# Full-row matmuls in the first token product, and one value product in each double step without scores

## The chip, the cores and the metric

The kernel runs on one core of a Trainium2 chip. The metric is the device time of one execution in microseconds (us), the median of three runs; lower is better. Five engines work side by side, each through its own queue in order: PE (TensorE, matmuls; the profile lists its weight loads as PEld), DVE (VectorE), ACT (ScalarE), POOL (GpSimd) and SP, which here only issues DMAs.

## The reference

Attention with the heads mixed before and after the softmax, then one token-and-channel MLP block on its output. Four batches, 12 heads, 448 positions, 64 elements a head, 768 channels.

```python
scores = scale * np.matmul(q, k.transpose(0, 1, 3, 2))
scores = np.einsum('bhij,hg->bgij', scores, w_pre)
attn = softmax(scores)                                  # over j, with 1e-9 added to the sum
attn = np.einsum('bhij,hg->bgij', attn, w_post)
x = np.matmul(attn, v)                                  # laid out as (batch, position, 768)
h = np.maximum(x.transpose(0, 2, 1) @ w_tok1, 0.0) @ w_tok2      # 448 -> 256 -> 448
u = x + h.transpose(0, 2, 1)
out = u + np.maximum(u @ w_ch1, 0.0) @ w_ch2                     # 768 -> 1536 -> 768
```

All data are float32.

## The kernel before

**Attention.** The 448 rows of a batch are cut into tiles T of 120, 120, 120 and 88 rows, 16 tiles in all. A tile's scores (`qk`, six calls a tile, two heads each) go to SBUF, and DMAs regroup them (`regroup`, to tile `r`) so that one group holds ten rows of all heads. A *step* takes two groups through `pre` (head mixing), `mx` (negated row maximum on DVE), `ex` (exponentials on ACT, two halves), `rec` (reciprocal on DVE, then two multiplications on POOL, lines 196 and 199), `post` (head mixing after the softmax, PE) and `turn` (a 32 by 32 transpose on DVE into the tile's `at` buffer, of which there are two). When all steps of a tile are turned, three calls of `av(T, hp)` make its value product on PE, with a copy on ACT (line 247), an addition on POOL (line 249) and a store.

**Double steps.** The main loop runs over 45 double steps J. Each issues six stages of steps that overlap: `post` and `turn` of steps `pa`, `pb`, `ex` and `rec` of `ea`, `eb`, `pre` and `mx` of `na`, `nb`. A planner (lines 469 to 488) sets ahead of time which `qk` and which `av` calls belong to which J: `score[J]` and `value[J]`. The engines' order is written out by hand and has two forms, chosen by the line quoted below. With scores in J, or with neither scores nor values, the first form is taken (lines 526 to 559): both `post` first, `av` last. With values but no scores the second form is taken (lines 561 to 582): `post(pa)`, `pre(na)`, then `av` between the exponentials of `eb` and `rec(eb)`, and then `post(pb)` and `pre(nb)`.

```python
        if qs or not vs:
```

The products `qk`, `post` and `av` share two PSUM buffers of the tag `w`; `pre` has two of its own. A product can begin only when the reader of the buffer's former content (the copy on ACT, or `turn` on DVE) is done.

Scores end at J = 38. Of the last double steps, 38 holds two value products of tile 12 and two score calls, 39 holds nothing, 40 one value product of tile 13, 41 two, 42 nothing, 43 one of tile 14 and 44 two. Tile 15 has its value products behind the loop.

**Weight conversion.** The MLP weights come as float64 bits and are split on the chip into a high and a low float32r part. `tok_tick` does the first token weight during J = 29 to 40. `cv_tick` does the rest unit by unit from J = 41 on (52 units; lines 432, 436 and 442 on DVE, 408 and 423 on ACT, 414 on POOL, 440 on POOL or, in the channel stage, on DVE). It is spread over the token stage and the first batch of the channel stage.

**Token stage.** For each batch: `tok1(b)`, `tr(b + 1)`, `tok2(b)`. `tr` transposes x on PE and splits it on ACT (line 606) and DVE (line 608, eight instructions a batch) into `xn` high and low. `tok1` has four groups (two halves of the channels, two of the 256 hidden units). A group is three times three matmuls of 128 rows (lines 616 to 618: high by high, high by low, low by high) for rows 0 to 383, and two matmuls for the last 64 rows: the tile `xn[0][:, 3]` holds the low part of those rows in partitions 0 to 63 and the high part in 64 to 127, and `w[0][:, 3]` holds the high weights twice, so line 630 makes high by high and high by low in one matmul of 128 rows. Line 631 makes low weights by high x from partitions 64 to 127 alone. `relu_split` follows on ACT (line 612) and DVE (line 613). `tok2` adds its product to x on DVE (line 649).

**Channel stage.** For each batch and each of 12 chunks c: `ch1` (18 matmuls), `relu_split` (lines 612 and 613, tiles `rh` and `rl`), three conversion units in batch 0, and `ch2` of the chunk before (18 matmuls), which reads `rl`.

Of the kernel before, what the change touches and what calls it, by code (L numbers as in the profile page):

```python
# [14 lines left out]
ALU = mybir.AluOpType  # L15
# [21 lines left out]
def attn_mixer_kernel(  # L37
# [12 lines left out]
    nc = tc.nc  # L50
    f32 = lambda ap: ap.bitcast(F32)
# [11 lines left out]
    def en(name, **kw):  # L63
        p = tc.alloc_tile_pool(name=name, reuse_waits="tile", **kw)
        opens[name] = p
        return p
# [27 lines left out]
    for b in range(B):  # L94
        for t in range(4):
            n = IT[t][1]
# [4 lines left out]
    NT = len(first)  # L101
# [28 lines left out]
    def pair(tag, name):  # L130
        return (ps if tag == "pre" else ps_w).tile([128, 2, 512], F32, tag=tag, bufs=2, name=name)
# [150 lines left out]
    for i in range(WARM):  # L282
        p = pair("w", "pw")
# [3 lines left out]
    for x in range(2):  # L287
        ps_ = slice(64 * x, 64 * x + 64)
        nc.vector.tensor_tensor(
            out=kpre[ps_, :60].rearrange("p (i g) -> p i g", i=5),  # L290
            in0=kcat[0][ps_, :12].unsqueeze(1).to_broadcast([64, 5, H]),
            in1=mask[0][ps_, 5 * x:5 * x + 5].unsqueeze(2).to_broadcast([64, 5, H]), op=ALU.mult,
# [3 lines left out]
    for s in range(2):  # L296
        ps_ = slice(64 * s, 64 * s + 64)
        for hf in range(2):
            nc.gpsimd.tensor_tensor(
                out=kpost[ps_, 32 * hf:32 * hf + 30].rearrange("p (g i) -> p g i", g=6),  # L300
                in0=kcat[1][ps_, 12 + 6 * hf:18 + 6 * hf].unsqueeze(2).to_broadcast([64, 6, 5]),
                in1=mask[1][ps_, 5 * s:5 * s + 5].unsqueeze(1).to_broadcast([64, 6, 5]), op=ALU.mult,
# [9 lines left out]
    prep = {}  # L312
# [5 lines left out]
    a1 = en("a1", bufs=1, side="right")  # L318
    cvt = en("cvt", bufs=2, side="right")
    prep["t1"] = [a1.tile([128, JT, DT], F32R, name=f"t1{i}") for i in range(2)]  # L320
    toks = [(w_t1[:, 512 * j:512 * (j + 1)], DT, [y[:, j, :] for y in prep["t1"]]) for j in range(JT)]
    tok_t = {}

    def tok_tick(t):
        i, odd = divmod(t, 2)
        if odd == 0:
            if 0 <= i < len(toks):
                src, n, _ = toks[i]
                r = cvt.tile([128, n, 2], I32, tag="r", bufs=3, name="tk_r")
                nc.sync.dma_start(out=r, in_=src.rearrange("p (n two) -> p n two", two=2))  # L330
                tok_t[i] = [r]
            i -= 2
            if 0 <= i < len(toks):
                r, g, a = tok_t[i]
                nc.scalar.copy(out=toks[i][2][0], in_=a)
            i += 1
            if 0 <= i < len(toks):
                g = cvt.tile([128, toks[i][1]], F32, tag="g", name="tk_g")
                nc.scalar.activation(out=g, in_=f32(tok_t[i][0])[:, :, 1], func=ACTF.Abs)
                nc.gpsimd.tensor_scalar(  # L340
                    out=g, in0=g, scalar1=MAG_MIN, scalar2=MAG_MAX, op0=ALU.max, op1=ALU.min,
                )
                tok_t[i].append(g)
        else:
            i -= 1
            if 0 <= i < len(toks):
                r, g = tok_t[i]
                a = cvt.tile([128, toks[i][1]], F32, tag="a", name="tk_a")
                ri, gi, ai = [y.bitcast(U32) for y in (r, g, a)]
                nc.vector.tensor_scalar(  # L350
                    out=gi, in0=gi, scalar1=3, scalar2=0x3FFFFFFF,
                    op0=ALU.logical_shift_left, op1=ALU.bitwise_and,
                )
                nc.vector.scalar_tensor_tensor(
                    out=ai, in0=ri[:, :, 1], scalar=0xC0000000, in1=gi, op0=ALU.bitwise_and, op1=ALU.bitwise_or,
                )
                nc.vector.scalar_tensor_tensor(
                    out=ai, in0=ri[:, :, 0], scalar=29, in1=ai, op0=ALU.logical_shift_right, op1=ALU.bitwise_or,
                )
                tok_t[i].append(a)  # L360
            i -= 1
            if 0 <= i < len(toks):
                hi, lo = toks[i][2]
                nc.gpsimd.tensor_tensor(out=lo, in0=tok_t.pop(i)[2], in1=f32(hi), op=ALU.subtract)

    def open_prep():
        close("cvt")
# [79 lines left out]
    def cv_tick(k, eng=nc.gpsimd):  # L447
        for _ in range(k):
            i = cv_pos[0]
            if i >= cv_lim[0]:  # L450
                return
            if i + 5 < len(units):
                cv_load(i + 5)
            cv_step(i, eng)
            if 0 <= i + 2 < len(units):
                cv_clamp(i + 2)
            if 0 <= i + 3 < len(units):
                cv_abs(i + 3)
            cv_pos[0] += 1
# [4 lines left out]
    sf = [f // 2 for f in first]  # L464
# [3 lines left out]
    value = {J: [] for J in range(-2, ND)}  # L468
    for T in range(NT - 1):
        J = (sl[T] + 1) // 2  # L470
        n = min(3, sf[T + 2] // 2 - J)
        for hp in range(3):
            value[J + min(hp, n - 1)].append((T, hp))
    for h in range(HP):
# [4 lines left out]
    for T in range(2, NT):  # L479
        hi = (sf[T] - 8) // 2  # L480
        lo = max((sl[T - 2] - 8) // 2 + 1 + (T == 4), hi - 2)
# [16 lines left out]
    for b in range(1, B):  # L498
        for h in range(0, HP, 2):
            J = uses[4 * b, 0] - 5 + h // 2  # L500
# [9 lines left out]
    for J in range(-2, ND):  # L510
# [49 lines left out]
        else:  # L560
# [20 lines left out]
            if na:  # L581
                ex(na, 0)
        tok_tick(J - JC)
        if J >= ND - 4:
            cv_tick((2, 1, 1, 1)[J - ND])
# [8 lines left out]
    def tr(b, hfs=(0, 1)):  # L594
        x = XR[b]
        xn = XN.get(b) or [a2.tile([128, JT - i, DM], F32R, tag=f"xn{i}", bufs=1, name=f"xn{i}") for i in range(2)]
        for hf in hfs:
            for j in range(JT):
                p = pst.tile([128, 512], F32, tag="tr", name="tr")
                for d in range(3):  # L600
                    nc.tensor.transpose(
                        out=p[:, 128 * d:128 * d + 128], in_=x[hf][:, d, min(128 * j, 320):min(128 * j, 320) + 128],
                        identity=prep["ident"],
                    )
                cs = slice(384 * hf, 384 * hf + 384)
                nc.scalar.copy(out=xn[0][:, j, cs], in_=p[:, :384])
                lo_t, r = (xn[1][:, j, cs], 0) if j < 3 else (xn[0][:64, 3, cs], 64)
                nc.vector.tensor_tensor(out=lo_t, in0=p[r:, :384], in1=f32(xn[0])[r:, j, cs], op=ALU.subtract)
        XN[b] = xn

    def relu_split(p, h, l):
        nc.scalar.activation(out=h, in_=p, func=ACTF.Relu)  # L612
        nc.vector.scalar_tensor_tensor(out=l, in0=p, scalar=0.0, in1=f32(h), op0=ALU.max, op1=ALU.subtract)  # L613

    def mm3(p, a, x, first, last):
        nc.tensor.matmul(out=p, lhsT=a[0], rhs=x[0], start=first, stop=False)  # L616
        nc.tensor.matmul(out=p, lhsT=a[0], rhs=x[1], start=False, stop=False)  # L617
        nc.tensor.matmul(out=p, lhsT=a[1], rhs=x[0], start=False, stop=last)  # L618

    def tok1(b):  # L620
        xn = XN[b]
        h1 = [a3.tile([128, 2, DM], F32R, tag=f"h1{i}", bufs=1, name=f"h1{i}") for i in range(2)]
        for hf in range(2):
            for m in range(2):
                p = psa.tile([128, 512], F32, tag="t", bufs=4, name="pt1")
                cs = slice(384 * hf, 384 * hf + 384)
                w = [y[:, :, 128 * m:128 * m + 128] for y in prep["t1"]]
                for j in range(3):
                    mm3(p[:, :384], [y[:, j] for y in w], [y[:, j, cs] for y in xn], j == 0, False)
                nc.tensor.matmul(out=p[:, :384], lhsT=w[0][:, 3], rhs=xn[0][:, 3, cs], start=False, stop=False)  # L630
                nc.tensor.matmul(out=p[:, :384], lhsT=w[1][64:, 3], rhs=xn[0][64:, 3, cs], start=False, stop=True)
                relu_split(p[:, :384], h1[0][:, m, cs], h1[1][:, m, cs])
                if b == hf == m == 0:
                    tr(0, (1,))
                if hf + m == 1 if b == 0 else hf == 0:
                    cv_tick(1)
        H1[b] = h1
# [49 lines left out]
    for b in range(B):  # L687
        tok1(b)
        if b + 1 < B:
            tr(b + 1)  # L690
        tok2(b)
# [93 lines left out]
```

## Time and profile before

| | |
|---|---|
| median of 3 runs | 773.65 us (773.21 to 775.1) |
| profiled execution, whole / its span | 778.99 us / 777.2 us |
| granted TensorE clock over the span | 0.999 |
| PE / DVE / ACT / POOL busy share of the span | 97% / 55% / 42% / 44% |
| attention (to about 337 us) / token stage / channel stage (from about 416 us) | 337 / 79 / 361 us |

The busy shares are means over stages that differ: DVE, ACT and POOL are near their limits up to about 500 us and nearly idle behind it. A matmul's duration includes its run through the array, so matmuls overlap, and what one costs is the distance of its start to the next start, not its duration. The idle time in square brackets at the end of a row is that of the row's engine just before it, with what ended it.

### The profile page before, as it was taken

How to read it: one execution, taken by the hardware profiler on the slowest of the kernel's cores; microseconds unless marked ns; L12 is line 12 of the kernel's file. 1: busy time of each engine (PE TensorE's matmuls, PEld its weight loads, DVE VectorE, ACT ScalarE, POOL GpSimd, SP SyncE). 2: the span in 40 equal slices, each digit the busy share in tenths (PEclk: the TensorE clock that was granted, in tenths of full speed). 3: DMA queues.
4: the chain of work that ended last, by engine and by line, in shares of the span. 5: the costliest groups of instructions: out<-in, count | busy, mean ns of one | idle time of the engine just before them, and what ended most of it. 6: DMA issues, size and time to landing. Idle time of an engine off the chain costs nothing.

```text
span 777.2 us, 21834 instructions
## 1 busy us (share of the span) xinstructions
PE 753.9 (97%) x9209; PEld 565.3 (73%) x9209; DVE 430.9 (55%) x749; ACT 329.9 (42%) x732; POOL 339.9 (44%) x342
## 2 busy tenths in 40 slices
PE   7899999999999998899999999999999999999997
PEld 2354565455555455578888999999999999999997
DVE  3776667666767978687999999620004000230002
ACT  2777777677777775455453445300002000200000
POOL 3676677667767778856668676100000000000000
PEclk9999999999999999999999999999999999999999
DMA  6776676466747633735656565330003000010001
GB/s 165 251 234 214 215 219 210 158 220 205 223 168 235 204 140 144 243 110 183 237 178 195 166 180 163 143 142 1 1 1 141 1 1 0 1 72 1 0 1 72
DMA packets 62755, 105.66 MB, mean 136 GB/s; under 512 B 21012, under 2 KB 49601, under 8 KB 62145
## 3 DMA queue, kind: packets, MB, share of 16 engines
q1 hardware_dynamic: 62160, 103.35, 41.0%
q8 instruction: 73, 1.20, 0.6%
q10 hardware_dynamic: 400, 0.87, 0.4%
q14 instruction: 26, 0.20, 0.1%
q0 software_dynamic: 96, 0.03, 0.0%
HBM read 49.18 MB, written 16.52 MB: 85 GB/s over the span
## 4 chain that ended last, share of the span: by engine, by line
PE 87%; DVE 6%; POOL 2%; ACT 2%; DMA 1%; issue 1%; SPq 0%; DVEq 0%; POOLq 0%; ACTq 0%
PE av L240 9%; PE post L208 9%; PE pc L616 8%; PE pc L617 8%; PE pc L618 8%; PE po L616 8%; PE po L617 8%; PE po L618 8%; PE qk L143 7%; PE pre L165 7%; DVE at L222 3%; PE pt L616 3%; PE pt L617 2%; PE pt L618 2%; POOL e L199 1%
## 5 line engine op out<-in xcount | busy, mean ns | idle before, releaser
L613 DVE SCALAR_TENSOR_TENSOR rl<-pc,rh 128x448 fp32r<-128x448 f32 x48 | 29.8, 622 | 227.4 <-ACT rh L612 227.4
L199 POOL TENSOR_TENSOR e<-e,sm 128x896 f32<-128x896 f32 x90 | 151.4, 1682 | 7.0
L222 DVE STREAM_TRANSPOSE at<-post 128x1024 f32<-128x1024 f32 (+1 forms) x98 | 112.0, 1150 | 66.5 <-PE post L208 66.3
L612 ACT ACTIVATE rh<-pc 128x448 fp32r<-128x448 f32 x48 | 26.1, 543 | 242.0 <-PE pc L618 242.0
L149 ACT COPY s<-qk 120x896 f32<-120x896 f32 (+1 forms) x91 | 82.2, 906 | 81.5 <-PE qk L143 80.1
L182 ACT ACTIVATE e<-pre,sm 128x448 f32<-128x448 f32 x180 | 112.9, 640 | 8.5 <-DVE sm L173 4.2
L616 PE MATMUL pc<-u,w 128*128 128x448 f32 x288 | 106.0, 368 | 0.0
L617 PE MATMUL pc<-u,w 128*128 128x448 f32 x288 | 106.0, 368 | 0.0
L616 PE MATMUL po<-rh,w 128*128 128x448 f32 x288 | 106.0, 368 | 0.0
L617 PE MATMUL po<-rl,w 128*128 128x448 f32 x288 | 106.0, 368 | 0.0
L618 PE MATMUL po<-rh,w 128*128 128x448 f32 x288 | 106.0, 368 | 0.0
L618 PE MATMUL pc<-u,w 128*128 128x448 f32 x288 | 106.0, 368 | 0.0
L173 DVE TENSOR_REDUCE sm<-pre 128x2 f32<-128x896 f32 x90 | 94.4, 1077 | 10.2 <-PE pre L165 10.1
L208 PE MATMUL post<-e,kpost 64*32 64x256 f32 x2880 | 91.8, 381 | 6.6 <-POOL e L199 5.6
L143 PE MATMUL qk<-k,q 64*64 64x448 f32 (+2 forms) x768 | 90.4, 544 | 5.5 <-DVE sm L191 3.6
L165 PE MATMUL pre<-r,kpre 64*64 64x448 f32 (+1 forms) x720 | 87.9, 549 | 3.2 <-ACT e L182 2.1
L414 POOL TENSOR_SCALAR cv_g<-cv_g 128x384 f32<-128x384 f32 (+1 forms) x52 | 82.4, 1585 | 18.1 <-ACT cv_g L408 18.1
L240 PEld LDWEIGHTS av<-at,v 64*64 64x64 f32 x2688 | 74.0, 132 | 18.5 <-ACT s L149 9.9
L240 PE MATMUL av<-at,v 64*64 64x120 f32 (+1 forms) x2688 | 77.8, 261 | 1.0 <-issue 0.7
L208 PEld LDWEIGHTS post<-e,kpost 64*32 64x32 f32 x2880 | 47.0, 106 | 41.6 <-POOL e L199 17.2
L143 PEld LDWEIGHTS qk<-k,q 64*64 64x64 f32 (+2 forms) x768 | 27.5, 128 | 54.1 <-DVE sm L191 30.4
L196 POOL TENSOR_TENSOR e<-e,sm 128x128 f32<-128x128 f32 x90 | 36.1, 401 | 70.0 <-DVE sm L194 32.7
(78 smaller groups left out, 1005.0 us busy)
## 6 DMA issues: line engine op xcount, KB each, us to landing
r<-s SPq DMA_DIRECT2D x172, 210.0 KB
cv_r<-in_w_ch_dram SPq DMA_DIRECT2D x48, 384.0 KB
v<-in_v_dram SPq DMA_DIRECT2D x16, 384.0 KB
xr<-x_dr SPq DMA_DIRECT2D x8, 672.0 KB
u_dr<-u SPq DMA_DIRECT2D x24, 224.0 KB
ur<-u_dr SPq DMA_DIRECT2D x4, 1344.0 KB
out_dram<-ur SPq DMA_DIRECT2D x24, 224.0 KB
x_dr<-x SPq DMA_DIRECT2D x36, 120.0 KB
```

Source lines behind the costliest of these rows:

```text
L143: nc.tensor.matmul(out=p[c:c + m, s, :S], lhsT=Q[T][r, h, c:c + m], rhs=K[b][r, h, :], start=True, stop=True)
L165: nc.tensor.matmul(out=p[64 * s:64 * s + 64, x, :S], lhsT=kpre[k], rhs=rt[a % NR][k], start=True, stop=True)
L173: nc.vector.tensor_reduce(out=s[:m, 0:2], in_=PP[st[0]][:m, :, :S], axis=AX.X, op=ALU.max, negate=True)
L182: nc.scalar.activation(out=E[st[0]][:m, x, :S], in_=p[:m, x, :S], func=ACTF.Exp, bias=s[:m, x:x + 1], scale=1.0, accum_out=s[:m, 2 + 2 * x ...
L199: nc.gpsimd.tensor_tensor(out=e[:m, :, :S], in0=e[:m, :, :S], in1=w.to_broadcast([m, 2, S]), op=ALU.mult)
L208: nc.tensor.matmul(out=p[32 * a:32 * a + 32, s, 256 * hf:256 * hf + 256], lhsT=kpost[k, 32 * hf:32 * hf + 32], rhs=ek[k, :, :, a, :], star ...
L222: nc.vector.transpose(out=AT[T][:, c:c + s1 - s0].rearrange("p c f -> p (c f)"), in_=p[:, s0:s1].rearrange("p c f -> p (c f)"),)
L240: nc.tensor.matmul(out=p[64 * s:64 * s + 64, r, 10 * w * u:10 * w * (u + 1)], lhsT=V[b][k, 6 * u + h, j, :], rhs=at_[k, u, :w, :, f:f + 5] ...
L414: nc.gpsimd.tensor_scalar(out=g[:P], in0=g[:P], scalar1=MAG_MIN, scalar2=MAG_MAX, op0=ALU.max, op1=ALU.min,)
L616: nc.tensor.matmul(out=p, lhsT=a[0], rhs=x[0], start=first, stop=False)
L617: nc.tensor.matmul(out=p, lhsT=a[0], rhs=x[1], start=False, stop=False)
L618: nc.tensor.matmul(out=p, lhsT=a[1], rhs=x[0], start=False, stop=last)
```

## The change

Three edits. The third is the planner's.

1. Partitions 0 to 63 of the low part of the last token weight, `prep["t1"][1][:64, 3]`, are set to zero once by POOL at the start; the split that writes this tile later leaves them alone (it writes partitions 64 to 127 for j = 3).
2. The matmul of line 631 takes all 128 partitions in place of the last 64. The first 64 meet the zero weights.
3. In the planner, the number n of double steps over which the three value products of a tile are spread grows by one where the tile that will reuse the `at` buffer begins with the second step of a double step, and only behind the last scores. `av(12, 2)` moves from J = 38 to 39, and `av(13, 2)` from J = 41 to 42. Nothing else in the plan moves. As 39 and 42 now hold a value product, they take the second form of the double step.

```diff
     prep["t1"] = [a1.tile([128, JT, DT], F32R, name=f"t1{i}") for i in range(2)]
+    nc.gpsimd.memset(f32(prep["t1"][1])[:64, 3], 0.0)
...
                 hi, lo = toks[i][2]
-                nc.gpsimd.tensor_tensor(out=lo, in0=tok_t.pop(i)[2], in1=f32(hi), op=ALU.subtract)
+                r = slice(64 if i == 3 else 0, 128)
+                nc.gpsimd.tensor_tensor(out=lo[r], in0=tok_t.pop(i)[2][r], in1=f32(hi)[r], op=ALU.subtract)
...
         J = (sl[T] + 1) // 2
-        n = min(3, sf[T + 2] // 2 - J)
+        n = sf[T + 2] // 2 - J
+        if sf[T + 2] % 2 and sf[T + 2] // 2 > (sf[NT - 1] - 8) // 2:
+            n += 1
+        n = min(3, n)
         for hp in range(3):
             value[J + min(hp, n - 1)].append((T, hp))
...
-                nc.tensor.matmul(out=p[:, :384], lhsT=w[1][64:, 3], rhs=xn[0][64:, 3, cs], start=False, stop=True)
+                nc.tensor.matmul(out=p[:, :384], lhsT=w[1][:, 3], rhs=xn[0][:, 3, cs], start=False, stop=True)
```

## Rows read from the trace of the kernel before

**Rows 1.** Page, part 1: engine, busy us, share of the span, instructions.

```profile
PE 753.9 (97%) x9209; PEld 565.3 (73%) x9209; DVE 430.9 (55%) x749; ACT 329.9 (42%) x732; POOL 339.9 (44%) x342
```

**Rows 2.** Busy time by stretch: length; PE, PEld, DVE, ACT, POOL; clock, DMA, GB/s.

```profile
280.31:288.43 8.12, 7.09 (x157) 3.63 (x153) 7.41 (x12) 5.08 (x13) 5.66 (x6) 1.00 0.43 161
288.43:296.74 8.31, 8.24 (x212) 5.34 (x209) 6.97 (x11) 6.14 (x16) 7.27 (x8) 1.00 0.38 141
296.74:301.81 5.07, 3.64 (x82) 1.48 (x81) 4.08 (x10) 2.42 (x7) 3.53 (x6) 1.00 0.30 98
301.81:308.06 6.25, 5.50 (x137) 3.05 (x137) 4.46 (x9) 4.63 (x14) 5.12 (x6) 1.00 0.48 181
308.06:315.02 6.96, 6.96 (x196) 4.57 (x192) 4.79 (x9) 3.71 (x11) 6.57 (x9) 1.00 0.40 116
315.02:320.36 5.34, 3.87 (x85) 1.51 (x81) 5.14 (x10) 1.39 (x5) 3.82 (x4) 1.00 1.01 334
320.36:330.86 10.50, 9.28 (x296) 6.70 (x297) 5.27 (x9) 5.04 (x14) 8.60 (x10) 1.00 0.65 231
371.00:391.00 20.00, 19.72 (x105) 16.57 (x102) 19.26 (x34) 9.85 (x22) 13.00 (x10) 1.00 0.68 238
```

**Rows 3.** Waits in sum: total us, times, longest; PE from 288 to 337 us.

```profile
PE post L208 <- POOL e L199: 2.9, 3, 1.4
PE post L208 <- DVE sm L191: 0.9, 1, 0.9
```

**Rows 4.** Groups by line: busy us, mean ns of one, idle before.

```profile
L199 POOL TENSOR_TENSOR e<-e,sm 128x896 f32<-128x896 f32 x90 | 151.4, 1682 | 7.0
L173 DVE TENSOR_REDUCE sm<-pre 128x2 f32<-128x896 f32 x90 | 94.4, 1077 | 10.2 <-PE pre L165 10.1
...
L631 PE MATMUL pt<-xn,t 64*128 64x384 f32 x16 | 7.1, 441 | 0.0
```

**Rows 5.** Timeline of PE in `tok1(1)`: start, us, engine, line.

```profile
360.19 0.33 PE L618 MATMUL pt<-xn,t 128*128 128x384 f32 x1
360.36 0.34 PE L630 MATMUL pt<-xn,t 128*128 128x384 f32 x1
360.63 0.44 PE L631 MATMUL pt<-xn,t 64*128 64x384 f32 x1
361.00 0.45 PE L616 MATMUL pt<-xn,t 128*128 128x384 f32 x1
361.28 0.34 PE L617 MATMUL pt<-xn,t 128*128 128x384 f32 x1
```

**Rows 6.** Timeline of PE's weight loads in the same stretch.

```profile
360.19 0.19 PEld L630 LDWEIGHTS pt<-xn,t 128*128 128x128 f32 x1
360.63 0.18 PEld L631 LDWEIGHTS pt<-xn,t 64*128 64x128 f32 x1 [0.25 <-issue]
```

**Rows 7.** Timeline of PE at the end of `tok1(1)` and in `tr(2)`.

```profile
367.61 0.44 PE L631 MATMUL pt<-xn,t 64*128 64x384 f32 x1
367.99 1.53 PE L601 MATMUL tr<-ident,xr 128*128 128x128 f32 x12
369.75 2.06 PE L601 MATMUL tr<-ident,xr 128*128 128x128 f32 x12 [0.24 <-DVE xn L608]
```

**Rows 8.** Timeline of DVE, token stage and first channel chunk: rows with idle time.

```profile
343.59 0.56 DVE L613 SCALAR_TENSOR_TENSOR h<-pt,h 128x384 fp32r<-128x384 f32 x1 [0.20 <-ACT h L612]
...
368.62 0.56 DVE L613 SCALAR_TENSOR_TENSOR h<-pt,h 128x384 fp32r<-128x384 f32 x1 [0.58 <-ACT h L612]
...
409.15 0.56 DVE L613 SCALAR_TENSOR_TENSOR h<-pt,h 128x384 fp32r<-128x384 f32 x1 [0.16 <-ACT h L612]
410.05 0.62 DVE L649 TENSOR_TENSOR u<-pt,xr 128x448 f32<-128x448 f32 x1 [0.34 <-PE pt L618]
...
421.76 0.61 DVE L613 SCALAR_TENSOR_TENSOR rl<-pc,rh 128x448 fp32r<-128x448 f32 x1
```

**Rows 9.** Timeline of PE, first matmul of the first `ch2`.

```profile
423.45 0.37 PE L616 MATMUL po<-rh,w 128*128 128x448 f32 x1
```

## The prediction

> **What bounds the kernel now.** I read the page first: PE is busy for 97% of the span [rows 1], so a gain must either make PE's own work shorter or remove some of the little time in which PE waits. The change tries both, in two different stages, so I read each stage by itself. For the value products that is the table of busy time by stretch [rows 2], cut at the starts of the double steps: its second to seventh rows are J = 38, 39, 40, 41, 42, and 43 with 44. The reader is to see PE's busy time beside the length. In 38 and 41, which hold two value products, PE is busy throughout (8.24 of 8.31, 6.96 of 6.96). In 39 and 42, which hold none, it waits for 1.43 and 1.47 us, in 40 for 0.75, in 43 and 44 for 1.22. Over the 42.43 us from 288.43 to 330.86 that makes 4.94 us of waiting. The list of waits says for whom: mostly POOL's multiplication of line 199 ahead of `post`, and once DVE ahead of `post` [rows 3]. So the work is there, in the wrong double steps.
>
> For the token product I read PE's own timeline [rows 5, 6]. PE has no idle time there, yet the starts are uneven: 0.17 us from one matmul of 128 rows to the next, but 0.27 into line 631, 0.37 from it to the next group's first matmul, and 0.28 from that to the second. The weight load of line 631 begins only with its matmul, 0.25 us after the load before it had ended, while that of line 630 began 0.17 us ahead of its matmul. The matmul of 64 rows stops the overlap on both its sides. Then I read DVE in that stage, since it splits what PE produces: from 371 to 391 us it is busy for 19.26 of 20.00 us [rows 2]. That decides how much of a faster PE arrives.
>
> **Part 1, the value products.** Removed: one product from J = 38 and one from 41. Added: one in 39 and one in 42, which thereby take the second form. No work is added. A product costs PE 6.96 - 5.50 = 1.46 us (41 against 40, which differ by one) [rows 2]. J = 38 then takes 8.31 - 1.46 = 6.85. J = 39 to 42 are each like J = 40: PE 5.50, DVE 4.46, ACT 4.63, POOL 5.12 us of work [rows 2]. If PE is the bound in each, they take 4 x 5.50 = 22.0, together 28.85 against 31.93 now (the sum of the five lengths): 3.1 us.
>
> Can PE be the bound? I walked the second form through. `pre(na)` needs ACT to be through with `ex(ea, 1)`, which now follows one copy and one exponential and not, as in 39 and 42 now, both `mx` of the double step (1.08 each [rows 4]). `post(pb)` needs POOL's `rec(eb)` of the double step before; that now stands behind the addition of the value product, which waits for `av` and its copy. In J = 40 one `post` and one `pre` take half of 5.50 - 1.46, 2.0 us, so `av` ends at about 3.5 us. The copy, the addition and the two multiplications (the last alone 1.68 [rows 4]) follow; I estimate 3.5 us for the four, from POOL's 5.12 less the 2.1 or so of `rec(ea)` and with the copy. POOL is then done at 7.0, that is 1.5 us into the next double step, where `post(pb)` comes at 3.5. So the wait that is added on POOL has about 2 us of cover; when that is gone, `post(pb)`, its transposition and the next `mx` come later one for one. `turn(pb)` of 39 and 42 writes the `at` buffer that the moved product reads; the product stands ahead of `post(pb)` on PE, so this wait is over when it is asked for. The store of the moved product goes one double step later, behind `regroup` of 39 on SP (in 42 there is none left); its data is next read in the token stage. The regrouping DMAs of 39 and 40 wait for the same `pre` as now and have one whole double step to land.
>
> J = 43 now begins after a wait for POOL, counted above, and then waits 0.9 us for DVE, which did `mx` twice in a row at the end of 42 [rows 3]; in the second form one of the two is done earlier. I take 0.5 us from the 0.9. Part 1: 3.1 + 0.5 = **3.6 us**. Bounds: above, all 4.94 us of waiting. Below, J = 37, which also has one product but with scores and the first token weight's DVE work, took 8.12 us with 7.09 of PE [rows 2]: 1.03 us of waiting. If each of the four had that, part 1 would be 3.6 - 4.1 = -0.5. I take 3.6, since J = 40 and 41 are the same form and lie nearest.
>
> **Part 2, the token product.** Per group, line 630 to the next group's second matmul takes 0.27 + 0.37 + 0.28 = 0.92 us [rows 5]; at 0.175 each it would take 0.53: 0.39 us less. There are 16 groups (x16 [rows 4]): 6.2 us. Four of them are followed by a transposition, 0.38 us after line 631 [rows 7]; no row shows one behind a matmul of 128 rows, so there the gain lies between 0.1 (the 0.27 alone) and 0.39, and PE's own gain between 5.1 and 6.2. The zero rows cost nothing in the matmul: it is as long as line 630, 0.34 us against 0.44. POOL's clearing of the zeros is one instruction ahead of the loop, shorter than its 1.68 us for 896 elements [rows 4], with PE waiting for nothing of it.
>
> The rows show that loads of 128 rows do run ahead of the matmul before them [rows 6], 0.17 us early for line 630. The Trainium skill (TensorE: Matmul & The Clock Gate, Part 3: Packing small matmuls) says that a weight load overlaps with running matmuls only when its row group differs from theirs, which speaks against this edit, since all row groups would be in use. By that rule part 2 would be 0 and the sum 3.6; the trace here disagrees with it.
>
> How much arrives? DVE works without a gap except for the few idle times of [rows 8], so those, and not PE's gain, are what batches 0 to 2 can give. `tr(b + 1)` can't end before DVE's line 608, so each batch is a meeting point. Batch 0: 0.20 and one more of 0.16 (rows of 0.16 stand for three). `tok2(0)` is PE's; then the first group of batch 1 ends 0.2 earlier (0.10 from its start, 0.10 from its length), and 0.58 idle follows. Batch 2: 0.16. At that meeting point the gain is 0.36 + 0.2 + 0.58 + 0.16 = 1.30 us, where PE alone would have had about 4 from its twelve groups. Batch 3 ends in no transposition, so its 4 x 0.39 = 1.56 go on to the channel stage: 2.86 for PE. DVE has 0.16 + 0.34 more to give: 1.80. The first `ch2` starts at 423.45 [rows 9] and needs DVE's line 613, which ends at 421.76 + 0.61 = 422.37 [rows 8]: 1.08 us of slack, so DVE allows 1.80 + 1.08 = 2.88. Part 2: **2.9 us** of about 6. Bounds: above 6.2, if DVE's order has more room than its gaps show; below 1.1, if DVE's gaps stay and only the slack ahead of `ch2` is used. I take 2.9, which both sums give.
>
> Behind that, PE runs the channel stage alone and nothing else changes. **Sum:** 3.6 + 2.9 = 6.5 us. Against the profiled execution 778.99 - 6.5 = 772.5; its span is 777.2, so 1.8 us lie around it. It stands 5.3 us above the median of the runs, and nothing of the sum hangs on that difference: 773.65 - 6.5 = **767.2 us**.
>
> **The rivals.**
> - *The token gain arrives whole.* Against it: DVE's 19.26 of 20 us. For it: busy time is no proof of need, and DVE's instructions could turn out shorter in another order. With 5.8, between 5.1 and 6.2: 773.65 - 3.6 - 5.8 = 764.3.
> - *The double steps gain nothing*: the new ones wait as 37 does, for POOL or DVE. Only part 2 remains: 773.65 - 2.9 = 770.8.
> - *Nothing but the last slack*: the double steps gain nothing, and DVE takes all of part 2 but 1.1: 772.6.
> - *The load of 128 rows isn't pulled ahead* at line 631, for the row groups are all in use. Part 1 alone: 770.1. Against it, line 630 sixteen times.
> - *Slower: POOL becomes the bound of 39 to 42.* The added addition holds up `rec(eb)`, hence `post(pb)`, `turn(pb)`, the next `mx` and `ex`, and so the next `av`: a ring. Each double step would be as long as 37, 8.12 us, or longer: 6.85 + 4 x 8.12 = 39.3 against 31.93, +7.4, less 2.9: 778.1. It decides once a double step exceeds (31.93 + 2.9 - 6.85) / 4 = 7.0 us. Against it: POOL's 5.12 us in 40 are below PE's 5.50, and 41 with two additions took 6.96 with no wait.
> - *The change doesn't do what it says*: the moved product stays in one lump or the matmul stays at 64 rows. The planner's condition holds for tiles 12 and 13 alone (tiles 14 and 15 begin at steps 79 and 85, both odd and behind the scores), so I give this no chance of its own.
>
> **How the numbers follow.** Forecast 0.52 (its own range 765.0 to 769.0), whole token gain 0.17, no gain in the double steps 0.15, only the last slack 0.08, load not pulled ahead 0.03, slower 0.05. The range 763.5 to 771.0 leaves out the last slack, the slower case, and some 0.06 at the edges of the others. What a measurement of this kernel can tell from no change is about 0.3%, 2.3 us. Faster by more (under 771.3): 0.52 + 0.17 + 0.03 + 0.11 of the 0.15 = 0.83. Within: the other 0.04 and 0.08 = 0.12. Slower: 0.05.
>
> **What would show it.** In the profile after: line 631 as 128 by 128 at 0.34 us, with starts 0.17 to 0.18 apart around it. Double steps 39 to 42 at about 5.5 us each, 38 at about 6.9, and the first token matmul about 3.6 us earlier than 337.07. DVE without idle time from the first split of batch 1 on, and longer waits of PE in `tr` for line 608, about 0.5 to 1 us per batch where now it is 0.24 [rows 7]. The first `ch2` about 6.5 us earlier than 423.45. The prediction is wrong if 39 to 42 show PE waiting for line 199 as now, or if `tr` waits no longer than now, which would mean that DVE had room that I didn't see.

## The result

The changed kernel takes 766.81 us in the median against 773.9 us, a ratio of 0.9913 (95% interval 0.9895 to 0.9931). Measured once more on another occasion it was 768.32 against 774.63, 0.9931 (0.9911 to 0.9951). So it is faster by 0.5% to 1.05%, 4 to 8 us; the forecast was 767.2, 6.5 us less than 773.65.

The profiled executions differ by more, 777.2 against 765.0 us of span, and a table of stretches shows why. A runs from the start of J = 38 to the first token matmul, B from there to the first matmul of the second channel product `ch1(0, 1)`, C from there to the end. The second profiles come from the experiments below (runs 6 and 10).

| us | before | before, second profile | after | after, second profile |
|---|---|---|---|---|
| A | 48.64 | 48.88 | 45.22 | 46.32 |
| B | 82.66 | 82.53 | 79.94 | 80.88 |
| C | 357.5 | 350.7 | 350.8 | 357.6 |
| A + B | 131.30 | 131.41 | 125.16 | 127.20 |

What the change did stands in A and B: 6.1 us less in the first profile of the changed kernel (3.4 and 2.7), but only 4.1 to 4.2 in its second. Run 10 tells where the 2.0 us between these two lie. C was not edited; it comes in two lengths, 6.8 us apart, with either kernel (last section), so the comparisons below go by A and B.

**A, the double steps.** The busy time by stretch of the changed kernel: length, then busy time of PE, PEld, DVE, ACT and POOL, clock, DMA share, GB/s. The rows are J = 38 to 42, and 43 with 44, as in [rows 2].

```profile
289.10:295.91 6.81, 6.73 (x155) 3.83 (x153) 5.54 (x9) 5.51 (x15) 6.19 (x7) 1.00 0.38 138
295.91:301.68 5.77, 5.52 (x139) 3.06 (x136) 5.01 (x11) 4.26 (x13) 5.03 (x7) 1.00 0.41 149
301.68:307.11 5.43, 5.43 (x141) 3.04 (x137) 4.87 (x9) 3.45 (x11) 4.81 (x5) 1.00 0.49 175
307.11:312.57 5.46, 5.46 (x140) 3.07 (x136) 4.79 (x9) 3.15 (x10) 5.16 (x7) 1.00 0.33 96
312.57:318.04 5.47, 5.47 (x141) 3.07 (x137) 4.81 (x10) 3.13 (x10) 5.31 (x7) 1.00 0.92 307
318.04:328.13 10.09, 9.41 (x300) 6.77 (x296) 5.62 (x9) 3.87 (x11) 8.52 (x10) 1.00 0.78 284
```

PE's busy time equals the length in 40, 41 and 42. What is left of its waits from 288 to 334 us, total, times and longest:

```profile
PE av L240 <- issue: 0.7, 1, 0.7
PE post L208 <- DVE at L222: 0.4, 1, 0.4
PE av L240 <- DVE at L222: 0.3, 1, 0.3
PE pre L165 <- ACT e L182: 0.3, 1, 0.3
```

The 2.9 us for POOL's line 199 of [rows 3] are gone, and the 0.9 for DVE are 0.4. J = 38 to 42 take 28.94 us in place of 31.93. Of all that is compared here this repeats best: 28.90 to 28.94 us in all seven profiles with the new plan, 31.91 to 31.93 in three of the four with the old plan and the old form (33.49 in run 5).

**B, the token product.** From the token stage on, line numbers of the changed kernel are five higher (631 is 636, 608 is 613, 649 is 654). PE's timeline in `tok1(1)` and at its end, to be laid beside [rows 5, 7]:

```profile
355.46 0.34 PE L621 MATMUL pt<-xn,t 128*128 128x384 f32 x1
...
357.05 0.33 PE L635 MATMUL pt<-xn,t 128*128 128x384 f32 x1
357.22 0.33 PE L636 MATMUL pt<-xn,t 128*128 128x384 f32 x1
357.40 0.33 PE L621 MATMUL pt<-xn,t 128*128 128x384 f32 x1
357.57 0.33 PE L622 MATMUL pt<-xn,t 128*128 128x384 f32 x1
...
362.94 0.34 PE L636 MATMUL pt<-xn,t 128*128 128x384 f32 x1
363.12 1.47 PE L606 MATMUL tr<-ident,xr 128*128 128x128 f32 x12
365.52 2.07 PE L606 MATMUL tr<-ident,xr 128*128 128x128 f32 x12 [0.93 <-DVE xn L613]
```

All starts around line 636 are 0.17 to 0.18 us apart, into the transposition too. The weight load of line 636 now runs 0.17 us ahead of its matmul, as that of line 630 did in [rows 6]:

```profile
357.05 0.19 PEld L636 LDWEIGHTS pt<-xn,t 128*128 128x128 f32 x1
```

`tok1(1)` with its 44 matmuls takes 363.12 - 355.46 = 7.66 us where it took 367.99 - 358.77 = 9.22, from this row of the kernel before to the transposition of [rows 7]: 1.56 less, 0.39 a group.

```profile
358.77 0.34 PE L616 MATMUL pt<-xn,t 128*128 128x384 f32 x1
```

Yet B is only 2.7 us shorter, not 6.2. PE's timeline shows the difference as waits. Four rows of DVE's timeline follow; 358.18 is the last one with idle time:

```profile
346.17 2.07 PE L606 MATMUL tr<-ident,xr 128*128 128x128 f32 x12 [1.28 <-DVE xn L613]
...
385.45 2.06 PE L606 MATMUL tr<-ident,xr 128*128 128x128 f32 x12 [1.52 <-DVE xn L613]
...
414.26 0.47 PE L621 MATMUL pc<-u,w 128*128 128x448 f32 x1 [0.66 <-DVE u L654]
```

```profile
338.40 0.56 DVE L618 SCALAR_TENSOR_TENSOR h<-pt,h 128x384 fp32r<-128x384 f32 x1 [2.93 <-ACT xn L611]
...
345.57 4.17 DVE L613 TENSOR_TENSOR xn<-tr,xn 128x384 fp32r<-128x384 f32 x8
...
358.18 0.56 DVE L618 SCALAR_TENSOR_TENSOR h<-pt,h 128x384 fp32r<-128x384 f32 x1 [1.83 <-ACT h L617]
...
413.59 0.62 DVE L654 TENSOR_TENSOR u<-pt,xr 128x448 f32<-128x448 f32 x1
```

PE waits for the splits of `xn` in all three batches, 1.28, 0.93 and 1.52 us where it was 0.24 as in [rows 7] in the last two and this, in the kernel before, in the first:

```profile
349.48 2.07 PE L601 MATMUL tr<-ident,xr 128*128 128x128 f32 x12 [0.34 <-DVE xn L608]
```

It also waits for 0.66 us ahead of `ch1(0, 1)`, a wait that the kernel before did not have. From 358.18 on DVE has no idle time up to the channel stage.

### The profile page after: what moved, and what is told of

Same layout as the page of the kernel before. It is cut to its first block, busy times and chain, and to the rows that moved or that the text cites. A ratio compares the mean times of both kernels' runs of the same rounds, so it can differ in the third digit from the quotient of the medians.

```text
span 765.0 us, 21842 instructions
## 1 busy us (share of the span) xinstructions
PE 741.5 (97%) x9209; PEld 566.7 (74%) x9209; DVE 429.1 (56%) x749; ACT 329.0 (43%) x732; POOL 340.2 (44%) x343
```

## The experiments

The theory is that of the prediction: PE is the bound in the new double steps, and DVE holds back more than half of the token gain. A and B are the stretches of the table above. The line numbers of the runs differ by their edits; the tile's name tells which instruction is meant.

**1. The planner's edit alone.** Line 631 stays as it was.

```diff
-        n = min(3, sf[T + 2] // 2 - J)
+        n = sf[T + 2] // 2 - J
+        if sf[T + 2] % 2 and sf[T + 2] // 2 > (sf[NT - 1] - 8) // 2:
+            n += 1
+        n = min(3, n)
```

> The planner's edit alone; line 631 stays a matmul of 64 rows. Gap theory (PE is the bound in the new double steps, DVE holds back most of the token gain): 3.4 us faster than before (ratio 0.9956), the stretch from the start of J = 38 to the first token matmul 45.2 us as after the change, the token stage as before. Rival (the token product carries nearly all of the gain and the double steps little): about 1.3 us faster or no difference (0.998 to 1.000).

Measured: 769.97 against 773.35 us, ratio 0.9938 (0.9912 to 0.9964). A is 45.61 us, 3.0 to 3.3 less than in the two profiles of before, B 82.63, as before. J = 38 to 42 take 28.93 us. PE's waits in the token stage are those of before:

```profile
PE tr L604 <- DVE xn L611: 0.8, 3, 0.3
```

So part 1 is worth 3.0 to 3.4 us by the stretch and the medians, and all of it lies in A.

**2. The zero rows alone.** Edits 1 and 2 of the change; the planner stays as it was. Of edit 2:

```diff
-                nc.tensor.matmul(out=p[:, :384], lhsT=w[1][64:, 3], rhs=xn[0][64:, 3, cs], start=False, stop=True)
+                nc.tensor.matmul(out=p[:, :384], lhsT=w[1][:, 3], rhs=xn[0][:, 3, cs], start=False, stop=True)
```

> The zero rows alone; the value products stay where they were. Gap theory: 2.7 us faster than before (ratio 0.9965), PE waiting for 3 to 4 us in all for DVE in the transpositions and for 0.5 to 0.8 us ahead of the second product of the channel stage. Rival (the token gain arrives whole): 5.8 us faster (0.9925). Second rival (the matmuls of the channel stage themselves became faster, 0.203 us apart in place of 0.207): in the profile here the channel stage is some 6 us shorter than before although none of it was edited.

Measured: 771.01 against 773.35 us, ratio 0.9948 (0.9918 to 0.9977). A is 49.21 us, as before within 0.6; B is 80.48, 2.0 to 2.2 less. The waits of PE from 334 to 430 us:

```profile
PE tr L603 <- DVE xn L610: 3.5, 3, 1.5
PE pc L618 <- DVE u L651: 0.9, 1, 0.9
```

The token gain does not arrive whole: 2.1 of 6.2 us, and 4.4 us of waits for DVE where before had 0.8. That it is less than the 2.7 of the first profile goes with a wait of DVE that this profile has and that one has not, 1.34 us for a store of `u` in the third batch (shown in run 10, which has it too). The two parts add up: 3.4 + 2.3 us in the medians against 6.3 and 7.1 for both, within what the intervals allow.

**3. The second form of the double step without the moved products.**

```diff
-        if qs or not vs:
+        if qs or not vs and J not in (39, 42):
```

> The kernel before with one edit: J = 39 and 42, which hold neither scores nor value products, take the second form of the double step; the value products stay two in 38 and two in 41. Gap theory, in which the moved products fill waits and the form removes some of them: about half of part 1, 1.5 to 2 us (ratio 0.9975), with 39 and 42 still ending in waits for POOL or DVE. Rival (the order of the second form alone makes the gain, the moved products only take their own time elsewhere): 3.4 us (0.9956). Second rival (only the filling counts): no difference, 39 at 5.1 and 42 at 5.3 us.

Measured: 771.69 against 773.15 us, but a ratio of 0.9995 (0.9972 to 1.0019): not told from no change by time. The trace tells more. A is 47.49 us, 1.2 to 1.4 less than before. Busy time by stretch, J = 39, then 42, then 43 with 44:

```profile
295.99:300.35 4.36, 4.01 (x83) 1.39 (x81) 3.17 (x8) 2.81 (x8) 3.47 (x5) 1.00 0.32 101
...
313.02:317.22 4.20, 3.96 (x84) 1.39 (x80) 3.99 (x9) 1.52 (x6) 3.76 (x3) 1.00 1.01 337
317.22:328.70 11.48, 9.65 (x296) 6.79 (x296) 6.33 (x11) 5.02 (x14) 8.69 (x10) 1.00 0.71 247
```

The form alone shortens the two empty double steps by 0.71 and 1.14 us, and 40 by 0.55 (5.70), 2.4 us in all, but 43 and 44 give 0.98 back. Of these, 0.52 is a wait of PE for nothing that the profile shows:

```profile
324.99 2.75 PE L240 MATMUL av<-at,v 64*64 64x120 f32 x92 [0.52 <-issue]
```

A wait of 0.68 us stands at the same place in the second profile of the changed kernel (run 10) and none in its first, so it is not put down to the form. The order is then worth 1.2 to 1.4 of the 3.4 us with this wait and 1.7 to 1.9 without it, and the products that fill it the rest. That is about what I expected of the form (1.5 to 2), and neither rival (3.4 or nothing) holds.

**4 and 5. DVE's load taken out of the token stage,** in the changed kernel and in the kernel before. For the weight units 4 to 19 the three DVE instructions are left out and ACT and POOL work on the clamped magnitudes.

```diff
-        g = prep["cv"].tile([128, n], F32, tag="cv_g", bufs=3, name="cv_g")
+        g = prep["cv"].tile([128, n], F32, tag="cv_g", bufs=4, name="cv_g")
...
+            dve = not 4 <= j < 20
+            if dve:
                 nc.vector.tensor_scalar(...)
                 nc.vector.scalar_tensor_tensor(...)
+            else:
+                a = gi.bitcast(F32)
...
+            if dve:
                 nc.vector.scalar_tensor_tensor(...)
```

> The changed kernel without the three DVE instructions (shift, sign, low bits) in the conversion of the 16 weight units that fall into the token stage, which therefore get wrong values; ACT's and POOL's parts of them are still done. About 29 us of DVE work are gone from the token stage. To be compared with the kernel before, treated alike. Gap theory: without DVE's limit the token gain arrives nearly whole, so this kernel is 3.4 + 5 to 6 = 8.5 to 9.5 us faster than the kernel before treated alike, and PE waits for DVE in the transpositions only for the 0.2 to 0.3 us that the splits themselves set. Rival (something else holds the gain back, ACT's splits or PSUM): the difference stays at 6 to 7 us.

> The kernel before without the same three DVE instructions for the same 16 weight units (wrong values for them). Both theories: as before within 1 us, since PE hardly waited for DVE in the token stage (0.8 us in the transpositions). If it is faster by more than 1 us, DVE held back the kernel before too, and my reading that PE alone bounds that stage was off.

Measured: the changed kernel without the load 764.09 against 773.35 us, 0.9863 (0.9815 to 0.991); the kernel before without it 776.27, 1.0027 (0.9985 to 1.0069). B is 77.16 and 82.27 us: the zero rows now bring 5.1 us instead of 2.7, and the kernel before gains 0.4 at most in B, so DVE did not hold it back. PE's waits from 334 to 430 us, first the changed kernel, then the kernel before:

```profile
PE tr L611 <- DVE xn L618: 1.6, 3, 0.9
```

```profile
PE tr L606 <- DVE xn L613: 0.6, 3, 0.2
```

5.1 us and the 1.0 us of waits that are still added make 6.1, PE's own gain (6.2 by the rows). A + B is 124.62 against 132.73 us, 8.1 less: somewhat under the 8.5 to 9.5 that I expected and above the rival's 6 to 7. (The medians are 12.2 us apart, but hold C; A + B is free of its two lengths.) The expectation that only 0.2 to 0.3 us of wait stay for each batch fell short by the 0.9 of the third. A is 47.46 and 50.46 us, about 2 us longer in both than in the kernels that they are made from, but not at the same place: in the first J = 43 and 44 took 13.38 us, in the second J = 40 took 7.83 in place of 6.25. Both have one more buffer for the magnitudes; whether that is the reason was not settled, so their difference in A, 3.0 us, is no clean second measure of part 1.

**6. The kernel before once more,** unchanged.

> The kernel before, unchanged, for a second profile of it. Both theories of the change: the stretches up to the channel stage as in the first profile, 48.6 us from the start of J = 38 to the first token matmul and 82.7 us from there to the second product of the channel stage. What it tells apart is the channel stage: if the matmuls there are 0.203 us apart, as in the profiles of the change and of its parts, the 0.207 of the first profile belonged to that execution and not to the kernel; if they are 0.207 again, the change made the channel stage faster too, by some 6 us.

Measured: 772.54 us in one timed execution; A 48.88, B 82.53, C 350.7 us. The stretches that the change touches repeat within 0.25 us; C, 357.5 in the first profile, does not. With the short C in a kernel that has none of the edits, the second rival of run 2 is out.

**7. Other PSUM banks for the first channel product.**

```diff
+    psc = en("psc", bufs=2, space=PSUM, side="right")
     psb = en("psb", bufs=1, space=PSUM)
...
-        p = psb.tile([128, 512], F32, tag="c1", bufs=2, name="pc1")
+        p = psc.tile([128, 512], F32, tag="c1", bufs=2, name="pc1")
```

> The changed kernel with the two PSUM buffers of the first channel product in a pool of their own, on the banks of the transpositions, which are free long before. Theory: PE's wait of 0.66 us ahead of the second product of the channel stage is for the last addition of the token stage (line 649 of before), which holds a bank that this product takes over; with other banks that wait is gone and the product comes 0.6 us earlier counted from the first token matmul (79.3 instead of 79.9 us). Rival (the wait is for DVE's queue as such, and only changes its place): the wait turns up at the first second-layer product, and nothing is gained there.

Measured: 765.45 us in one timed execution, B 79.20 us, 0.74 less than in the first profile of the changed kernel. `ch1(0, 1)` starts without a wait, and ahead of the addition that it had waited for:

```profile
413.00 0.36 PE L621 MATMUL pc<-u,w 128*128 128x448 f32 x1
```

```profile
413.14 0.62 DVE L654 TENSOR_TENSOR u<-pt,xr 128x448 f32<-128x448 f32 x1
```

So the wait was for the bank, and it did not move to the next product.

**8 and 9. The transpositions in two halves,** with the banks of 7, measured twice, the second time side by side with the changed kernel.

```diff
             if d % 3 == 2 and b + 2 < B:
                 load_x(b + 2, (d // 3,))
+            if d == 1 and b + 1 < B:
+                tr(b + 1, (1,))
...
         if b + 1 < B:
-            tr(b + 1)
+            tr(b + 1, (0,))
         tok2(b)
```

> The kernel of the other PSUM banks with the second half of each batch's transpositions moved behind the first two of the six products of the second token matmul, so that PE has work while DVE splits the first half. Theory (PE's waits in the transpositions, 3.7 us in all, are what DVE costs, and DVE still has idle time in batch 0 and 1): the wait of 1.28 us of the first batch is gained and kept, and 0.6 from the banks, 1.5 to 2 us faster than the changed kernel (ratio to before 0.989). Rival (DVE is full, so PE's wait only moves to a later point): at most the 0.6 us, ratio 0.991. If the transpositions among the products break PE's pace more than 0.3 us each time: no gain.

> The version with the split transpositions and the other PSUM banks, once more, side by side with the changed kernel. Theory (the waits of PE at the meeting points came from the order, PE and DVE standing at the same point, and not from a DVE that is full): faster than the changed kernel by the 4.0 us that the first profile shows from the start of J = 38 to the second product of the channel stage; ratio to before 0.986. Rival (the gain is given back behind that point): ratio 0.991, no faster than the changed kernel.

Measured: 763.1 against 773.15 us, 0.9889 (0.9852 to 0.9926), and 764.29 against 774.63, 0.9877 (0.9845 to 0.9909). The changed kernel beside it is the 768.32 us and 0.9931 of the first section. B is 75.85 and 75.92 us, 4.0 less than after the change, A 45.31 and 45.02, C 350.9 and 350.8. Waits of PE from 334 to 430 us, and DVE's idle times in the token stage, second time:

```profile
PE pt L621 <- DVE h L618: 0.7, 1, 0.7
PE tr L606 <- DVE xn L613: 0.4, 1, 0.4
```

```profile
337.55 0.56 DVE L618 SCALAR_TENSOR_TENSOR h<-pt,h 128x384 fp32r<-128x384 f32 x1 [2.24 <-ACT xn L611]
349.03 2.08 DVE L613 TENSOR_TENSOR xn<-tr,xn 128x384 fp32r<-128x384 f32 x4 [1.01 <-ACT xn L611]
353.85 0.63 DVE L654 TENSOR_TENSOR u<-pt,xr 128x448 f32<-128x448 f32 x1 [1.02 <-DMA u_dr<-u]
355.51 0.56 DVE L618 SCALAR_TENSOR_TENSOR h<-pt,h 128x384 fp32r<-128x384 f32 x1 [1.03 <-ACT h L617]
```

The gain is twice what I expected, and the rival that DVE is full and the wait only moves is out: PE's waits fell from 4.4 to 1.1 us with all of DVE's work in place. With the changed kernel's order PE and DVE stood still in turn. PE waited at the transpositions. DVE waited five times in the second token product of the first batch, for PE and then for POOL, and for 1.83 us at 358.18; of the changed kernel:

```profile
350.74 0.62 DVE L654 TENSOR_TENSOR u<-pt,xr 128x448 f32<-128x448 f32 x1 [0.35 <-PE pt L623]
...
353.26 0.62 DVE L654 TENSOR_TENSOR u<-pt,xr 128x448 f32<-128x448 f32 x1 [0.67 <-PE pt L623]
354.49 0.62 DVE L654 TENSOR_TENSOR u<-pt,xr 128x448 f32<-128x448 f32 x1 [0.60 <-POOL u L676]
```

With products to do in between, PE waits in one transposition only, and DVE's idle time from the first split of `xn` to the next batch's first split of `h` shrinks from 4.7 to 3.1 us. This version is about 10 us faster than the kernel before and, side by side, 4.0 us faster than the changed one, as expected of run 9.

**10. The changed kernel once more.**

> The changed kernel again, side by side with the version of the next run. Ratio to before 0.991 as in its first measurement; the waits of PE in the transpositions 3.7 us in all and 0.7 us ahead of the second product of the channel stage.

Measured: the ratio 0.9931 already told. PE's waits in the transpositions are 3.9 us in all, ahead of `ch1(0, 1)` 0.93; A 46.32, B 80.88, C 357.6 us. J = 38 to 42 take 28.90 us, as in the first profile. What A has more, 1.1 us, comes behind them, most of it in two waits of PE for nothing that the profile shows, 0.68 us in J = 44 and 0.32 in the transposition behind it. Of what B has more, 0.9 us, 0.7 comes behind a wait of DVE for a store of `u` (the second row below):

```profile
325.55 2.79 PE L240 MATMUL av<-at,v 64*64 64x120 f32 x92 [0.68 <-issue]
```

```profile
398.14 0.62 DVE L654 TENSOR_TENSOR u<-pt,xr 128x448 f32<-128x448 f32 x1 [1.30 <-DMA u_dr<-u]
```

Why the store was late in this execution and in run 2, and not in the first profile, was not found. So the gain in B with this order is 1.6 to 2.7 us, by the profile that is taken.

## Why the prediction was right, step by step

**Part 1, the value products: right, step by step.** The sum of 28.85 us for J = 38 to 42 came to 28.94: 6.81 for 38 (6.85 forecast), and 22.13 for the four others (22.0). In 40 to 42 PE is the bound, as worked out from the cost of J = 40. In 39 0.25 us remain for `ex`, at the change from the first form to the second. 43 with 44 gained 0.41 of the 0.5. In all 3.4 instead of 3.6 in the first profile; in the second, with its two waits behind J = 42, 2.3 to 2.6. The cover that was claimed for POOL's longer queue held: no wait for line 199 is left. The walk could not say how much the form brings and how much the filling; run 3 shows 1.2 to 1.9 for the form and the rest for the filling. Run 3 also shows the gain of the form being partly given back in 43 and 44, so the low bound of -0.5 had a ground, but the place was another than the one I named.

**Part 2, PE's own gain: right.** 0.39 us a group, and the transposition, for which no row existed, costs 0.18 us behind a matmul of 128 rows (bounds 0.17 to 0.38). So PE's own gain is at the upper end, 6.2 us by the rows, as runs 4 and 5 confirm (5.1 and 1.0 of waits, 6.1). The load of 128 rows is pulled ahead, by 0.17 us for line 636. By the rule of the Trainium skill (TensorE: Matmul & The Clock Gate, Part 3: Packing small matmuls), that a load overlaps only in another row group, B would not have moved, and run 2 moved it by 2.1 us.

**Part 2, what arrives: right in size, partly by luck, and wrong in two places.** Forecast were 2.9 us; 2.7 arrived in the first profile, 2.0 to 2.2 in run 2 and 1.6 to 1.8 in run 10, where DVE waited for a store. The following goes by the first profile. At the third meeting point the gain since the first token matmul was to be 1.30 us; it was 1.82 (4.57 at the start of `tok2(2)`, 391.84 to 387.27, less 2.75 at the first token matmul). All three terms were too small: batches 0 to 2 gave 0.56, 0.92 and 0.34 us in place of 0.36, 0.78 and 0.16. I took DVE's chain as fixed but for its gaps. In batch 0, from its first split to the transposition's, it took 348.87 - 340.85 = 8.02 us, and after the change 345.57 - 338.40 = 7.17, 0.85 less: its conversion instructions were shorter too, by about half a microsecond, for which no run shows the reason. But it began later behind the first token matmul, 4.08 us in place of 3.78, so 0.56 arrived.

```profile
340.85 0.56 DVE L613 SCALAR_TENSOR_TENSOR h<-pt,h 128x384 fp32r<-128x384 f32 x1 [2.24 <-ACT xn L606]
...
348.87 4.18 DVE L608 TENSOR_TENSOR xn<-tr,xn 128x384 fp32r<-128x384 f32 x8
```

In batches 1 and 2 the last two splits of `h` now follow each other directly, and from the first of them to the transposition's first split it is 0.72 and 0.29 us less, where the gaps were 0.58 and 0.16. Batch 3 brought its 1.56. PE's waits in the transpositions are 0.9 to 1.5 us, where I had named 0.5 to 1. The step that failed is the last one. I let the slack end at the first `ch2`, which needs DVE's line 613, with 1.08 us. The first wait is one product earlier: `ch1(0, 1)` takes over the PSUM bank that the last addition of the token stage reads. Before, that addition ended at 418.89 + 0.62 = 419.51 and the product began at 419.73: 0.22 us of slack, which I had not looked for.

```profile
418.89 0.62 DVE L649 TENSOR_TENSOR u<-pt,xr 128x448 f32<-128x448 f32 x1
```

```profile
419.73 0.37 PE L616 MATMUL pc<-u,w 128*128 128x448 f32 x1
```

Run 7 shows it by removing it. So 2.72 us arrived instead of 2.9; the two misses, +0.5 in batches 0 to 2 and -0.7 at the bank, nearly cancel, and that is luck.

**The rivals.** That the gain arrives whole is out (runs 2 and 4). That the double steps gain nothing is out (run 1). POOL as the bound is out (its 4.8 to 5.3 us stay below PE's 5.43 to 5.52). That DVE is nearly full was a right price for this order but a wrong cause in part: taking DVE's work away gives 2.8 us in B (run 4), and leaving it there in another order gives 4.0 with the banks (runs 8 and 9). DVE's 19.26 of 20 us was a fact of that stretch only. [rows 8] leaves out DVE's idle time in and behind the second token product of batch 0: in the kernel before five gaps of 0.34 to 0.66 us and one of 2.03 stand between 353 and 362 us, 4.8 us in all, while PE and POOL caught up. So "without a gap except for the few idle times of [rows 8]" did not hold there.

## What to carry to other kernels

In a stream of matmuls over all rows, one over half the rows cost its neighbours their overlap here, 0.39 us for each; filling the other half with zero weights removed that, and the place to read it is the distance of starts, since no idle time is shown. When a stage gets faster on one engine, list the points at which two engines meet and the slack at each, PSUM banks that pass from one stage to the next included, and count only what passes all of them. Before calling the second engine full, look whether it idles elsewhere in the same stage: then the order can be changed so that both keep working across the meeting point.

## What the runs showed of the hardware

The channel stage, 1728 matmuls of 128 by 448 that nothing delays, runs at two paces, with the same program. Of the kernel before, C was 357.5 us in one profile and 350.7 in the other; of the changed kernel 350.8 in one and 357.6 in the other. One group of its matmuls by line, the second profile of before and the second of the changed kernel:

```profile
L617 PE MATMUL po<-rl,w 128*128 128x448 f32 x288 | 105.2, 365 | 0.0
```

```profile
L622 PE MATMUL po<-rl,w 128*128 128x448 f32 x288 | 106.1, 368 | 0.0
```

The starts are 0.2027 us apart in the mean in the one case and 0.2067 in the other, with a granted clock of 0.999 to 1.000 in all four. What sets the pace was not found. All other profiles here had the shorter one. Nearly 7 us is as much as the whole change brings, so a comparison of two profiles by their spans would have told nothing; by the stretches that the change touches it did. Even there two profiles of one kernel differ by up to 1 us a stretch (run 10).
